# Seven block products for eight in the first FFN step of four groups: a fused linear attention and bilinear FFN kernel

## The chip, the cores and the metric

The kernel runs on one core of a Trainium2 chip. A core has a matrix engine (TensorE, in the profile PE, with its weight loads as PEld), three engines for elementwise work (VectorE or DVE, ScalarE or ACT, GpSimd or POOL), and queues that issue DMA transfers; nearly all transfers here are issued by the SP queue. Matrix products go to PSUM, which has eight banks of 128 x 512 float32; DVE and ACT read them from there. The metric is the time of one execution on the device in microseconds (us), lower is better. The kernel before takes 231.97 us (median of three executions, 231.74 to 232.61).

## The reference

Inputs are q, k, v of shape (4 batches, 8 heads, 768 positions, 64), one decay per head, and three FFN matrices. The attention goes over blocks of 64 positions and carries a state per head:

```
intra = (qb @ kb^T) * lam**(i-j), zero for j > i, then @ vb
inter = (qb * lam**(i+1)) @ kv_state
out   = intra + inter
kv_state = lam**64 * kv_state + (kb * lam**(63-j))^T @ vb
```

Its output, reordered to x with 3072 tokens and 512 columns, goes through a bilinear FFN with d_ff = 1536:

```
out = ((x @ w_a) * (x @ w_b)) @ w_out        # float32 result, 3072 x 512
```

## The kernel before, in words

**Units and groups.** The tokens are 24 blocks ("units" 0 to 23) of 128; a batch has six, and the attention state passes from unit to unit within a batch. `GROUPS` makes eight groups of 4, 1, 2, 4, 4, 4, 4 and 1 units. A group is what the FFN works on at a time: its x, transposed and in bfloat16, is the tile `xT` (four slices of 128 columns of d_model, by up to 512 tokens).

**The FFN of a group** (`ffn`). First step: for each of 12 chunks f of d_ff, four matmuls (one for each slice of d_model) accumulate `a_ps`, ACT casts it to `a_sb` (L477), four more accumulate `b_ps`, and DVE multiplies the two into `ab` (L495). The matmuls are on L468 and 512 columns wide in a group of four. Second step: for each unit t of the group, 12 matmuls over the chunks of d_ff (L515) give `op`, ACT copies it to SBUF (L510), and SP stores 128 rows of the output (L511). Rows of the first `KEEP_GROUPS` groups are kept in staging buffers instead (`o_kept`, L506) and stored later by a piece "W" (`store_kept`, L501).

**Attention pieces.** The attention of later units is done between the matmuls of the FFN. `hook(slot)` is called after each of the 12 chunks of the first step (slots 0 to 11) and after every half of an `op` in the second (slots from 12), and puts there what the written-out table `PLAN` says for the group:

- "P" (or its halves "PK" and "PV") prepares a unit: POOL multiplies k and q by powers of the decay (L276), one DMA transposes both into `qkT` (L304), and v is cast to `vb` (L295). The loads of a unit two or three further on are issued at the end of "P" (`pump`, `load_x`, L130).
- "S": eight small matmuls make the scores `kq0`, `kq1` (L332), and DVE masks them (L349, two instructions).
- "V": four matmuls update the state `kvd` (L396), and DVE copies its diagonal blocks out (`kv_copy`, L429).
- "O2", "Q": the outputs of two units (`inter` and `intra`, L366), their cast into the next group's `xT` on ACT (`evac_o`, L389), for the later units the state update too (L418), and for "Q" also the scores and masks of two more units.
- "W" stores a kept row, "C" casts a block of w_out, "T" transposes a unit on PE.

**What sets the order.** The order of all instructions is written out; each engine and the SP queue work through theirs in order, and wait on semaphores for data and for buffers. SP's order therefore mixes loads, transposes and stores: a transpose that waits for POOL holds up the loads behind it. POOL and SP run ahead of PE as far as buffers let them. PSUM has seven banks in rotation (`ps_bank`) and one for the state. Buffers that matter: `wst` (staging for weights, kept rows), `qkT`, `a_sb`, `o_sb`, and four each for raw q, k and v.

Of the kernel before, what the change touches and what calls it, by code (L numbers as in the profile page):

```python
# [22 lines left out]
def _bc(ap, dims):  # L23
# [5 lines left out]
W_CHUNKS = (256,) * 6  # L29
W_STEPS = ((0, 1), (2,), (3,), (4, 5))  # L30
W_HALVES = (4, 5)
W_BUFS = 12
LOOKAHEAD = {9: 2, 10: 1}
DMA_T = range(7, 24)
KEEP_GROUPS = 3
PACK = 4


# [2 lines left out]


PLAN = {
    0: [(0, "V", 3), (8, "C", 0), (9, "C", 1), (15, "C", 2), (18, "C", 3), (23, "PK", 4),
        (26, "C", 4), (26, "T", 4), (29, "C", 5), (29, "S", 4), (30, "PV", 4), (33, "O", 4),
        (35, "PK", 5), (35, "PV", 5)],
    1: [(0, "V", 4), (2, "T", 5), (3, "PK", 6), (6, "PV", 6), (6, "S", 5), (7, "T", 6),
        (10, "S", 6), (12, "O2", (5, 6)), (13, "P", 7)],
    2: [(0, "V", 6), (1, "P", 8), (4, "P", 9), (7, "V", 7),
        (9, "S", 7), (9, "S", 8), (6, "PK", 10), (10, "V", 8), (11, "PV", 10),  # L50
        (12, "Q", (7, 8, 9, 10)), (12, "P", 11), (13, "V", 9), (14, "P", 12),
        (14, "O2", (9, 10))],
    3: [(6, "S", 11), (6, "S", 12)],
}
for _g, _u in ((3, 11), (4, 15), (5, 19)):
    PLAN.setdefault(_g, []).extend(
        [(1, "P", _u + 2), (3, "P", _u + 3), (6 if _g == 3 else 4, "V", _u),
         (9 if _g == 3 else 7, "Q", (_u, _u + 1, _u + 2, _u + 3)), (10, "P", _u + 4),
         (12, "P", _u + 5), (13, "V", _u + 2), (16, "Q", (_u + 2, _u + 3, _u + 4, _u + 5))])
PLAN[3] += [(_s, "W", None) for _s in range(12, 19)]  # L60
PLAN[5] = [(_s, _n, (21, 22, 23) if _us == (21, 22, 23, 24) else _us)
           for _s, _n, _us in PLAN[5] if _us != 24]
PLAN[6] = [(4, "O", 23)]


@with_exitstack
def kernel(
# [11 lines left out]
    nc = tc.nc  # L79
# [13 lines left out]
    wst_pool = ctx.enter_context(tc.tile_pool(name="wst", bufs=W_BUFS))  # L93
    ld_pool = ctx.enter_context(tc.tile_pool(name="ld", bufs=4))
    prep_pool = ctx.enter_context(tc.tile_pool(name="prep", bufs=6))
    qkT_pool = ctx.enter_context(tc.tile_pool(name="qkT", bufs=5))
    msk_pool = ctx.enter_context(tc.tile_pool(name="msk", bufs=4))
    xT_pool = ctx.enter_context(tc.tile_pool(name="xT", bufs=2))
    a_pool = ctx.enter_context(tc.tile_pool(name="a", bufs=5))
    ab_pool = ctx.enter_context(tc.tile_pool(name="ab", bufs=2))  # L100
    o_pool = ctx.enter_context(tc.tile_pool(name="o", bufs=4))
    ps_pool = ctx.enter_context(tc.tile_pool(name="ps", bufs=1, space=PSUM))
    kvps_pool = ctx.enter_context(tc.tile_pool(name="kvps", bufs=1, space=PSUM))

    ctx.enter_context(tc.manual_schedule())


# [2 lines left out]
    def ps_bank(name, shape, dt, hold=False, ffn=False, at=None):  # L110
        i = bank["next"] if at is None else at
        while i in bank["held"] or (ffn and i == bank["ffn"]):
            i = (i + 1) % 7
        if ffn:
            bank["ffn"] = i
        bank["next"] = (i + 1) % 7
        if hold:
            bank["held"].add(i)
        return ps_pool.tile(shape, dt, name=name, tag=f"ps{i}")


    qr = q.rearrange("b h (nb p) d -> b nb p h d", p=BLK)
# [39 lines left out]
    def cast_w(kind, c, eng):  # L162
        t = staged.pop((kind, c))
        if kind == "o":
            dst = wo_sb[:, 2 * c:2 * c + 2, :]
        else:
            dst = w_part(wa_sb if kind == "a" else wb_sb, c)
        if eng == "act":
            nc.scalar.copy(dst, t)  # L169
        elif eng == "first":  # L170
            nc.vector.tensor_copy(dst[:, :3, :128], t[:, :3, :128])  # L171
            nc.gpsimd.tensor_copy(dst[:, 3:, :128], t[:, 3:, :128])
            nc.gpsimd.tensor_copy(dst[:, :, 128:], t[:, :, 128:])
        else:
            nc.vector.tensor_copy(dst, t)
        pump()

    pending = []
    for cs in W_STEPS:
# [8 lines left out]
    def pump():  # L188
        while pending:
            kind, c = pending[0]  # L190
            if kind in "abo":
                if len(staged) >= W_BUFS:
                    return
            elif c >= used["u"] + LOOKAHEAD.get(used["u"], 2 if used["u"] > 8 else 3):
                return
            pending.pop(0)
            if kind in "abo":
                load_w(kind, c)
            else:
                load_x(kind, c)  # L200
# [106 lines left out]
            U[u]["qT"], U[u]["kT"] = qkT[:, 0], qkT[:, 1]  # L307

    def prep_v(u):
        make_vb(u, "pool" if u < n0 + 3 else "dve")  # L310
        pump()

    def piece_T(u):
# [20 lines left out]
        return kq  # L334

    def masks(u, kq):
        ms = mask(kq)
        U[u]["m"] = lambda i, hp: ms[i][:, hp, :]

    def mask(kq, split=False):  # L340
# [94 lines left out]
    def piece_V(u):  # L435
        kv_update(u)
        if u % NB < NB - 1:
            kv_copy(u, kv["ps"])

    xTs = {}  # L440

    def pieces_O(us, nxt=()):
        kqs = [score_banks() for u in nxt]
        o_banks(us)
        for u, kq in zip(nxt, kqs):
            scores(u, kq)
        for u in us:
            inter(u)
        for b in range(2):
            for u in us:  # L450
                intra(u, b)
            evac_o(us, b)
        beside = len(us) == 2 and us[0] >= n0 + 5
        if beside:
            kv_beside(us[1])
        for u, kq in zip(nxt, kqs):
            masks(u, kq)
        if beside and us[1] % NB < NB - 1:
            kv_copy(us[1], kv["ps"])


    g_u0 = [sum(GROUPS[:i]) for i in range(len(GROUPS))]
# [36 lines left out]
    def store_kept():  # L499
        row, o_sb = kept.pop(0)  # L500
        nc.sync.dma_start(out=out_r[row], in_=o_sb)  # L501
# [66 lines left out]


    gx = {}  # L570

    def new_xT(g):
        gx[g] = xT_pool.tile([128, KS, 512], BF16, name="xT", tag="xT")
# [131 lines left out]
    for g, n in enumerate(GROUPS):  # L705
        if g + 1 < len(GROUPS):
            new_xT(g + 1)
        plan = {}
        for slot, name, us in PLAN.get(g, ()):
            plan.setdefault(slot, []).append((name, us))  # L710

        def hook(slot, plan=plan):
            for name, us in plan.get(slot, ()):
                if name == "C":
                    cast_w("o", us, "dve")
                elif name == "PK":
                    prep_k(us)
                elif name == "PV":
                    prep_v(us)
                elif name == "P":  # L720
                    prep_k(us)
                    prep_v(us)
                elif name == "W":
                    store_kept()
                elif name == "T":
                    piece_T(us)
                elif name == "S":
                    piece_S(us)
                elif name == "V":
                    piece_V(us)  # L730
                elif name == "O":
                    pieces_O((us,))
                elif name == "O2":
                    pieces_O(us)
                else:
                    pieces_O(us[:2], us[2:])

        ffn(g_u0[g], n, gx.pop(g), hook, g == 0, g + 1 == len(GROUPS))

# [1 line left out]
_INS = ['q', 'k', 'v', 'lam', 'moe_w_a', 'moe_w_b', 'moe_w_out']  # L741
# [26 lines left out]
```

## Time and profile before

| What | Value |
|---|---|
| Median of three executions | 231.97 us (231.74 to 232.61) |
| Span of the profiled execution, first to last instruction | 230.2 us |
| PE busy | 221.4 us, 96% |
| DVE, ACT, POOL busy | 118.2, 88.8, 49.9 us |
| Groups 3, 4, 5, 6 (first matmul to first matmul of the next) | 82.3, 117.6, 152.3, 187.0 to 218.8 us |
| Granted TensorE clock | 0.999 |

The time of the profiled execution itself is known by its span, 230.2 us; the 1.8 us up to the median lie around it. A page gives the busy time of each engine, the chain of waits that ended last, and groups of instructions with their mean duration and the idle time before them. The timeline gives instructions in order of time; a run of one line is merged into one row, with its count. "Releaser" is what ended a wait.

### The profile page before, as it was taken

The page shows a single profiled execution, that of the slowest core. Times are in us where ns is not written, and L with a number is a line of the kernel's source. Part 1 is how long each engine was busy: PE and PEld are TensorE (multiplying, and loading weights), DVE is VectorE, ACT ScalarE, POOL GpSimd, SP SyncE. Part 2 cuts the span into 40 slices and gives each one's busy share as a digit, 9 for nine tenths or more (in the row PEclk, how much of TensorE's full clock was granted, in tenths as well). Part 3 has the DMA queues.
Part 4 walks back from the last instruction along what each step waited for, and adds up shares of the span by engine and source line. Part 5 has one row for each costly group of instructions (what it writes and reads, how often), then busy time and mean ns, then how long its engine had stood idle before and what let it go on. Part 6 is the DMA issues. An engine that isn't in the chain of part 4 may idle for free.

```text
span 230.2 us, 4630 instructions
## 1 busy us (share of the span) xinstructions
PE 221.4 (96%) x1816; PEld 121.0 (53%) x1839; DVE 118.2 (51%) x205; ACT 88.8 (39%) x172; POOL 49.9 (22%) x65
## 2 busy tenths in 40 slices
PE   7699999999999999999999999999999999999994
PEld 2475444459688544454544454544454544444493
DVE  0994865736488845876416574426574313341050
ACT  2686563056433243242233342233342233432261
POOL 6061000228351436333302433002100000000000
PEclk9999999999999999999999999999999999999999
DMA  4999999999999999999979995249200220000211
GB/s 130 317 277 347 363 387 293 303 217 196 202 211 182 215 186 231 233 195 200 350 222 217 157 235 89 94 116 205 48 0 0 94 91 0 4 0 31 106 48 47
DMA packets 97542, 39.37 MB, mean 171 GB/s; under 512 B 85488, under 2 KB 92016, under 8 KB 97520
## 3 DMA queue, kind: packets, MB, share of 16 engines
q1 hardware_dynamic: 97232, 39.00, 75.2%
q8 instruction: 14, 0.23, 0.4%
q10 hardware_dynamic: 288, 0.07, 0.1%
q14 instruction: 8, 0.07, 0.1%
HBM read 28.32 MB, written 6.29 MB: 150 GB/s over the span
## 4 chain that ended last, share of the span: by engine, by line
PE 92%; DMA 3%; SPq 1%; issue 1%; ACT 1%; DVE 0%
PE a_ps L468 27%; PE b_ps L468 27%; PE op L515 27%; PE o_ps L366 5%; DMA k<-in_k_dram 3%; PE kq L332 3%; PE kvd L396 2%; SPq L224 1%; PE tps L318 1%; PE kq L633 1%; PE kv L396 0%; PE tk L597 0%; DVE scratch L587 0%; PE kvd L418 0%; ACT scratch L608 0%
## 5 line engine op out<-in xcount | busy, mean ns | idle before, releaser
L495 DVE TENSOR_TENSOR ab<-a_sb,b_ps 128x512 bf16<-128x512 bf16 (+2 forms) x96 | 52.2, 552 | 75.5 <-PE b_ps L468 55.1
L468 PE MATMUL a_ps<-xT,wa_sb 128*128 128x512 bf16 (+2 forms) x384 | 76.3, 322 | 0.6 <-ACT xT L389 0.3
L468 PE MATMUL b_ps<-xT,wb_sb 128*128 128x512 bf16 (+2 forms) x381 | 76.6, 325 | 0.2
L477 ACT CAST a_sb<-a_ps 128x512 bf16<-128x512 f32 (+2 forms) x96 | 45.2, 481 | 62.4 <-PE a_ps L468 60.0
L515 PE MATMUL op<-wo_sb,ab 128*128 128x512 bf16 (+2 forms) x300 | 63.9, 362 | 1.0 <-issue 0.6
L468 PEld LDWEIGHTS <-wb_sb 128*128 128x128 bf16 x384 | 34.5, 98 | 28.7 <-ACT wb_sb L169 0.2
L468 PEld LDWEIGHTS <-wa_sb 128*128 128x128 bf16 x392 | 34.4, 98 | 28.3 <-DVE wa_sb L171 0.5
L515 PEld LDWEIGHTS <-ab 128*128 128x128 bf16 x312 | 28.7, 98 | 29.9
L349 DVE TENSOR_TENSOR m<-kq,lotri 128x512 bf16<-128x512 f32 x47 | 29.3, 683 | 15.8 <-PE kq L332 15.7
L276 POOL TENSOR_TENSOR qk<-kf,lp_k 128x512 bf16<-128x512 f32 x18 | 18.8, 1042 | 73.9 <-DMA kf<-in_k_dram 60.7
L276 POOL TENSOR_TENSOR qk<-qf,lp_q 128x512 bf16<-128x512 f32 x20 | 21.9, 1097 | 22.6 <-DMA qf<-in_q_dram 22.6
L510 ACT COPY o_sb<-op 128x512 f32<-128x512 f32 (+2 forms) x19 | 10.3, 541 | 34.0 <-PE op L515 34.0
L389 ACT CAST xT<-o_ps 128x512 bf16<-128x512 f32 (+1 forms) x24 | 12.1, 555 | 17.5 <-PE o_ps L366 17.4
L429 DVE TENSOR_TENSOR st<-kvd,bdiag 128x512 bf16<-128x512 f32 x18 | 12.3, 683 | 3.2 <-PE kvd L396 3.2
L295 DVE CAST vb<-vf 128x512 bf16<-128x512 f32 x17 | 11.6, 682 | 3.8 <-DMA vf<-in_v_dram 3.7
L366 PE MATMUL o_ps<-m,vb 128*64 128x128 bf16 x192 | 8.0, 222 | 0.0
L208 PE MATMUL idle<-idle_sb 128*128 128x512 bf16 (+2 forms) x23 | 6.5, 411 | 1.3 <-DVE idle_sb L203 1.3
L295 POOL CAST vb<-vf 128x512 bf16<-128x512 f32 x7 | 4.3, 611 | 13.7 <-DMA vf<-in_v_dram 13.7
L320 ACT COPY qkT<-tps 128x1024 bf16<-128x1024 bf16 x3 | 3.0, 1012 | 10.6 <-PE tps L318 10.6
L332 PEld LDWEIGHTS <-qkT 64*128 64x128 bf16 x160 | 4.5, 94 | 4.2 <-issue 3.2
L332 PE MATMUL kq<-qkT 64*128 64x128 bf16 x160 | 6.6, 218 | 0.1
L366 PEld LDWEIGHTS <-vb 128*64 128x64 bf16 x192 | 5.8, 109 | 1.3
(58 smaller groups left out, 81.0 us busy)
## 6 DMA issues: line engine op xcount, KB each, us to landing
vf<-in_v_dram SPq DMA_DIRECT2D x24, 256.0 KB, 5.0
qf<-in_q_dram SPq DMA_DIRECT2D x20, 256.0 KB, 4.2
kf<-in_k_dram SPq DMA_DIRECT2D x20, 256.0 KB, 4.6
out_dram<-o_sb SPq DMA_DIRECT2D x16, 256.0 KB, 2.0
wst<-in_moe_w_a_dram SPq DMA_DIRECT2D x6, 512.0 KB, 8.6
wst<-in_moe_w_b_dram SPq DMA_DIRECT2D x6, 512.0 KB, 8.9
wst<-in_moe_w_out_dram SPq DMA_DIRECT2D x6, 512.0 KB, 10.6
out_dram<-o_kept SPq DMA_DIRECT2D x7, 256.0 KB, 4.0
```

Source lines behind the costliest of these rows:

```text
L276: eng_of(eng).tensor_mul(dst.rearrange("p (c b) d -> p b c d", b=2), x[:].rearrange("p (b c) d -> p b c d", b=2), lp.rearrange("p (b c) o ...
L295: eng_of(eng).tensor_copy(vb, vf)
L332: nc.tensor.matmul(kq[i][:, hp, :], lhsT=d["kT"][p, hp, :], rhs=d["qT"][p, hp, :], start=True, stop=True, skip_group_check=True)
L349: nc.vector.tensor_mul(m, kq[i], lotri_bc)
L366: nc.tensor.matmul(U[u]["o"][b][p, c // 2, :], start=new[b, h % 2], stop=True, skip_group_check=True, **ops)
L389: nc.scalar.copy(dst, src)
L429: nc.vector.tensor_mul(st[:].rearrange("p c b d -> p c (b d)"), ps[:].rearrange("p c b d -> p c (b d)"), bdiag_bc)
L468: nc.tensor.matmul(ps[:, lo:hi], lhsT=w_sb[:, s, f * 128:(f + 1) * 128], rhs=xT[:, s, lo:hi], start=(s == 0), stop=(s == KS - 1), skip_gro ...
L477: nc.scalar.copy(a_sb[:, :gt], ps[:, :gt])
L495: nc.vector.tensor_mul(ab[:, f, :gt], a_sb[:, :gt], ps[:, :gt])
L510: nc.scalar.copy(o_sb[:, lo:hi], op[:, lo:hi])
L515: nc.tensor.matmul(op[:, lo:hi], lhsT=ab[:, f, t * 128:(t + 1) * 128], rhs=wo_sb[:, f, lo:hi], start=(f == 0), stop=(f == FC - 1))
```

## The change

In groups 3 to 6 the first FFN step is no longer `ffn` but `ffn_z`. There xT is cut in two halves of 256 tokens and two halves of 256 columns of d_model, and w_a and w_b into two halves of d_model by two halves of d_ff. The product of two such 2 x 2 block matrices is formed from seven block products instead of eight. It needs sums of the blocks: four sums of each weight matrix, formed once (`weight_sum`, pieces "WS" in groups 0 and 1, eight DVE instructions), and three sums of each group's xT (`x_sums`, piece "X", three DVE instructions).

For each n of 6 (chunks n and n + 6 of d_ff at once) the seven products, each for a and b side by side in one bank (four matmuls of 256 columns), go into three banks: U takes products 1, 5, 3, 2 in turn, V takes 4 and 6, W takes 0. The banks are read while they grow: ACT copies U after product 1 (`u1`), V after product 4 (`v1`) and U after product 5 (`u2`) to SBUF; DVE forms three results as W - u1, U - v1 and V - u2; the fourth is U after product 2, cast by ACT; and one DVE multiplication of 1024 elements makes `ab` for both chunks. Product 2 and what follows it are issued one n later, inside the next one.

The second step has the same 48 matmuls, in another order: `out_part` takes first the chunks that are ready (5 and 11 last), in four banks.

Banks 0 to 4 belong to `ffn_z` in these groups, so that attention pieces there share banks 5 and 6. Buffers change: `wst` 12 to 8, `qkT` 5 to 4, `a_sb` 5 to 4, `o_sb` 4 to 3. `KEEP_GROUPS` goes from 3 to 2: five rows are kept, not seven, and stored in group 2 (slots 4, 10, 11, 12, 15), not in group 3. `PLAN` is written anew; "Q" is left in group 2 alone, and in groups 3 to 5 its parts stand as separate "S" and "O2". `KV_ENG` and `VB_ENG` say for each unit which engine copies its state and casts its v. The mask no longer has a split form in `masks`.

```diff
-W_BUFS = 12
+W_BUFS = 8
-KEEP_GROUPS = 3
+KEEP_GROUPS = 2
...
+    2: [(2, 'V', 6), (2, 'P', 8), (3, 'P', 9), (4, 'W', None), (5, 'V', 7), (5, 'PK', 10),
+        (7, 'V', 8), (8, 'S', 7), (8, 'S', 8), (10, 'V', 9), (10, 'W', None), (11, 'PV', 10),
+        (11, 'W', None), (12, 'P', 11), (12, 'W', None), (12, 'Q', (7, 8, 9, 10)),
+        (13, 'P', 12), (14, 'O2', (9, 10)), (15, 'X', 3), (15, 'P', 13), (15, 'W', None)],
+    3: [(0, 'S', 11), (2, 'P', 14), (4, 'S', 12), (7, 'S', 13), (7, 'P', 15),
+        (9, 'O2', (11, 12)), (11, 'S', 14), (11, 'V', 13), (15, 'P', 16),
+        (16, 'O2', (13, 14)), (16, 'X', 4), (17, 'P', 17), (17, 'P', 18), (17, 'S', 15),
+        (19, 'S', 16), (19, 'P', 19)],
...
+    def weight_sum(i):
+        kind, j = "ab"[i % 2], i // 2
...
+        if j == 0:
+            nc.vector.tensor_sub(z[:, 0], a22, a21)
+        elif j == 1:
+            nc.vector.tensor_sub(z[:, 1], a11, z[:, 0])
+        elif j == 2:
+            nc.vector.tensor_sub(z[:, 2], a12, z[:, 1])
+        else:
+            nc.vector.tensor_add(z[:, 3], a11, a21)
...
+    def x_sums(g):
...
+        nc.vector.tensor_sub(z_sub, xT[:, :, 0:256], xT[:, :, 256:512])
+        nc.vector.tensor_add(z_add, xT[:, 0:2, :], xT[:, 2:4, :])
+        nc.vector.tensor_add(z_mix, xT[:, 0:2, 0:256], xT[:, 2:4, 256:512])
...
+        def product(ps, n, i, fresh=False):
+            for k, kind in enumerate("ab"):
+                wt = lhs(kind, i)
+                for s in range(2):
+                    nc.tensor.matmul(ps[:, k, :], lhsT=wt[:, s, n * 128:(n + 1) * 128],
+                                     rhs=rhs[i][:, s, :], start=(fresh and k == 0 and s == 0),
+                                     stop=True, skip_group_check=True)
+
+        def snap(ps, tag):
+            t = wst_pool.tile([128, 2, 256], F32, name=tag, tag="wst")
+            nc.scalar.copy(t, ps)
+            return t
...
+        def finish(n):
+            d = P.pop(n)
+            product(d["U"], n, 2)
+            oab = d["oab"]
+            nc.scalar.copy(oab[:, 0], d["U"])
+            o5 = oab[:].rearrange("p (h t) k c -> p h t k c", h=2)
+            nc.vector.tensor_mul(
+                ab[:].rearrange("p (h i) (t c) -> p h i t c", h=2, t=2)[:, :, n],
+                o5[:, :, :, 0, :], o5[:, :, :, 1, :])
+
+        def begin(n):
+            d = P[n] = {}
+            d["U"] = z_bank("U", n % 2)
+            product(d["U"], n, 1, True)
+            d["u1"] = snap(d["U"], "u1")
+
+        for n in range(NP):
+            if n != 1:
+                begin(n)
+            d = P[n]
+            oab = d["oab"] = wst_pool.tile([128, 4, 2, 256], BF16, name="oab", tag="wst")
+            d["V"] = z_bank("V", 2 + n % 2)
+            product(d["V"], n, 4, True)
+            v1 = snap(d["V"], "v1")
+            hook(2 * n)
+            W = z_bank("W", 4)
+            product(W, n, 0, True)
+            nc.vector.tensor_sub(oab[:, 2], W, d["u1"])
+            product(d["U"], n, 5)
+            u2 = snap(d["U"], "u2")
+            if n:
+                finish(n - 1)
+            else:
+                begin(1)
+            product(d["V"], n, 6)
+            product(d["U"], n, 3)
+            nc.vector.tensor_sub(oab[:, 1], d["U"], v1)
+            nc.vector.tensor_sub(oab[:, 3], d["V"], u2)
+            hook(2 * n + 1)
...
+        out_part(0, early[:3])
+        finish(NP - 1)
+        out_part(0, early[3:])
+        hook(FC)
+        out_part(1, early)
```

## The prediction

> **What bounds the kernel now.** First the page's first part and the chain that ended last, which say that PE is the path.
>
> ```profile
> PE 221.4 (96%) x1816; PEld 121.0 (53%) x1839; DVE 118.2 (51%) x205; ACT 88.8 (39%) x172; POOL 49.9 (22%) x65
> PE 92%; DMA 3%; SPq 1%; issue 1%; ACT 1%; DVE 0%
> ```
>
> So time is won by taking PE work away, and lost by making PE wait. How long PE takes for a step is read from the chain in order of time: start, duration, count.
>
> ```profile
> 62.34 0.44 PE a_ps L468 x4
> ...
> 82.27 0.86 PE a_ps L468 x4
> ...
> 105.34 2.59 PE op L515 x12
> ```
>
> Four matmuls take 0.864 us at 512 columns (82.27 to 83.14) and 0.437 us at 256 (62.34, group 2): 216 and 109 ns each, so halving the width costs nothing extra. The third line is the second step, 216 ns a matmul. Then what DVE and ACT need, from the groups by shape (line, engine, tiles, count, busy us, mean ns; then the idle time before them):
>
> ```profile
> L349 DVE TENSOR_TENSOR m<-kq,lotri 128x512 bf16<-128x512 f32 x47 | 29.3, 683 | 15.8 <-PE kq L332 15.7
> ...
> L510 ACT COPY o_sb<-op 128x512 f32<-128x512 f32 x16 | 9.4, 585 | 32.1 <-PE op L515 32.1
> ...
> L495 DVE TENSOR_TENSOR ab<-a_sb,b_ps 128x256 bf16<-128x256 bf16 x12 | 5.0, 418 | 5.1 <-ACT a_sb L477 3.0 <-PE b_ps L468 1.8
> ...
> L587 DVE TENSOR_TENSOR scratch<-k,lp_k 128x512 bf16<-128x512 f32 x4 | 2.8, 692 | 0.3
> ```
>
> and how closely they follow each other, from the timeline:
>
> ```profile
> 34.69 2.04 ACT L477 CAST a_sb<-a_ps 128x512 bf16<-128x512 f32 x4
> ...
> 82.11 1.03 PE L468 MATMUL a_ps<-xT,wa_sb 128*128 128x512 bf16 x4
> 83.17 0.59 ACT L477 CAST a_sb<-a_ps 128x512 bf16<-128x512 f32 x1 [0.23 <-PE a_ps L468]
> ...
> 95.07 2.48 DVE L349 TENSOR_TENSOR m<-kq,lotri 128x512 bf16<-128x512 f32 x4
> ```
>
> A DVE instruction on 512 elements lasts 0.68, but four in a row take 2.48, so one starts (2.48 - 0.68) / 3 = 0.60 after the other; on ACT (2.04 - 0.59) / 3 = 0.49. ACT starts 0.20 after PE could go on (a_ps ends at 83.14, the next matmul began at 82.97). Last, the end of group 2 in the timeline:
>
> ```profile
> 70.05 1.23 SPq L304 DMA_TRANSPOSE qkT<-qk  x1
> ...
> 71.34 0.58 SPq L130 DMA_DIRECT2D qf<-in_q_dram  x1
> ...
> 78.65 2.00 SPq L304 DMA_TRANSPOSE qkT<-qk  x1
> ...
> 81.93 0.54 DVE L295 CAST vb<-vf 128x512 bf16<-128x512 f32 x1 [2.42 <-DMA vf<-in_v_dram]
> ```
>
> DVE waits there 2.42 us for unit 12's v; nothing on PE needs DVE then.
>
> **The change part by part.** *PE in the first step.* Before, 24 quartets of 0.864 = 20.73 us a group; after, 6 x 7 products of 0.437 = 18.35. Saved 2.38, in four groups **9.5 us**. The second step keeps its 48 matmuls, attention its own.
>
> *One n of the steady state*, from the durations above (t = 0 at product 1; 3.06 on PE if nothing waits). PE: U1 0 to 0.44, V4 to 0.87, W0 to 1.31, U5 to 1.75, the former n's U2 to 2.19, V6 to 2.62, U3 to 3.06. ACT: u1 0.64 to 1.22, v1 1.13 to 1.71, u2 1.95 to 2.53, the former U's cast 2.44 to 3.02. A release reaches PE about 0.05 later (DVE to PE at 10.77 and 10.82). U5 needs u1 at 1.27 and starts at 1.31; U3 needs u2 at 2.58 and starts at 2.62; the next U1 needs its bank at 3.07 and could start at 3.06. All fit, by 0.04 or -0.01. DVE: the multiplication starts at about 3.1, U - v1 0.6 later, done at 4.4; the next U2 needs it at 4.81: 0.4 to spare. ACT starts 4 x 0.49 = 1.96 in 3.06, DVE 4 x 0.60 = 2.4. Margins of 0.04 won't all hold; bounds 0 and 0.26 a cycle (a late read each at U5, U3 and U1, 0.05 to 0.1); taken 0.025 x 24 = **0.6** lost.
>
> *The multiplication* of 1024 bfloat16, both inputs in SBUF, is in no row. By bytes it is the float32 instruction of L587 (0.69), by elements 0.69 + 512 x 1.05 ns = 1.22 (1.05 is the slope from 0.418 at 256 to 0.684 at 512). I take 0.69: the nearest row with two SBUF inputs reads as many bytes. The same holds for x_sums (0.69, 0.69, 0.42) and the eight weight sums of 1536 (0.96 or 1.76).
>
> *The end of the first step.* U2 of the last n comes after three op matmuls, 0.65, not after 1.75, but needs U - v1 at 1.35 after U3's end: 0.70 late, less what the hook of slot 11 puts between (S14 and V13 0.5, S19 0.3, nothing, O 0.6): 0.2 + 0.4 + 0.7 + 0.1 = **1.4** lost. ab of chunks 5 and 11 is then 1.6 away, and 17 matmuls (3.7) cover it.
>
> *The start of group 3.* In the changed order z_sub stands on DVE behind the cast of unit 12's v, and V4, PE's second product, needs z_sub. In before v arrives at 81.93 and group 3 starts at 82.27. Two kept rows now stand in SP's queue before unit 11's loads: the first fits the wait before 70.05, the second moves the loads from 71.34 by about 0.5 (one of L501 issues in 0.52), and its 256 KB take some 0.7 of busy DMA. So v12 at 82.4 to 83.2, cast 0.42, z_sub 0.69: V4 at 83.6 to 84.3 in place of 82.7. Lost **1.2** (0.7 to 1.8; 0 if the stores find idle DMA, 4 if all five rows' 1.3 MB at 200 GB/s came before). S11, at slot 0, needs unit 11's transpose: issued at 78.65 + 0.5 to 1.2, and transposes land 3.1 to 5.9 later, median 4.3: 83.5 to 84.2, just inside the same stall. ACT likewise waits for unit 11's v at slot 12, ahead of xT's casts; PE needs those only at group 3, and ACT has 2 us to spare.
>
> *Attention in the first steps.* Each S adds 0.30 to PE and 1.2 to DVE, each O2 1.2 to PE and 1.0 to ACT. DVE starts in group 3 up to slot 10: 24 x 0.60, three S 3.6, one state copy 0.6: 18.6, against PE 20.5; groups 4 and 5, 18.5 and 18.0 against 21.6 and 20.4. There is room, but DVE instructions with both inputs in SBUF meet POOL:
>
> ```profile
> 91.24 1.32 DVE L295 CAST vb<-vf 128x512 bf16<-128x512 f32 x1 [1.27 <-DMA vf<-in_v_dram]
> ...
> 91.24 1.04 POOL L276 TENSOR_TENSOR qk<-qf,lp_q 128x512 bf16<-128x512 f32 x1
> ```
>
> That cast lasts 0.42 alone and 1.32 beside POOL. POOL's 22 of these for units 13 to 23 take 23 us of about 100, so some 4 of 18 multiplications wait about 0.7, of which 0.4 is spare (0 if none meet, 4 x 1.04 = 4 at most). With state copies on ACT before u1 (0.2 once): **1.2** lost. [...]
>
> *Groups 0 to 2.* Weight sums: in 39.6 to 53.5 DVE is busy 8.0 of 13.9 us, and five starts of 0.87 go in; two stand before the last w_out cast, which then ends at 43.6 + 2 x 0.87 + 0.7 = 46.0, while its matmuls start near 48; unit 5's k moves from 49.35 to 51.9, needed by a transpose at 52.9. In group 1 three more, between multiplications of 0.2 with four a_sb ahead. **0.3** lost; by elements, without this cover, 2.5. The smaller pools cost nothing: w_a's fifth block needs the buffer that POOL's cast frees at 18.7 and is issued at 21.0; eight transfers stay outstanding; uncovered, it would be one 512 KB block, 1.5. The stores leave group 3, where nothing waited for them.
>
> *Preparations* of units 13 to 23 move by up to a dozen slots, each with two POOL multiplications, a transpose on SP and three loads behind it. POOL and SP run ahead of PE as before. With four qkT buffers a transpose waits on SP for the outputs of the unit four before, and loads and stores stand behind it: unit 19's waits for slot 5 of group 4, takes 2.0 to issue and 4.3 to land, and S19 comes 9 us after that slot. The least room has S16 (slot 19; its transpose follows the store of slot 15), 6.7 us for 0.9 + 4.3. At nothing; if landing takes 5.9 or more there, up to 1.
>
> Sum: 9.5 - 0.6 - 1.4 - 1.2 - 1.2 - 0.3 = 4.8 saved. 230.2 - 4.8 = 225.4 span; the median lies 1.8 above the profiled span: **227.2**.
>
> **The rivals.** *A, slower: elements, not bytes.* If bfloat16 pairs go one by one, each multiplication takes 1.13 of DVE's starts, not 0.60. DVE then has 21.8, 21.7, 21.2 and 18.8 against PE's 20.5, 21.6, 20.4 and 18.7: with about 0.8 of filling each, some 5 lost; weight sums 2.2 and x_sums 0.5 more: 227.2 + 7.7 = **234.9**. It decides from 4.8 lost, about 0.95 a multiplication. For it: no DVE row here handles two bfloat16 SBUF inputs; against it: 1024 float32 are cast in 0.69 (L175). [...]
>
> *B, about the same: the reads are late.* If U5, U3 and U1 wait 0.07 each, the cycle is 3.27, not 3.06: 24 x 0.21 = 5 more than none, 4.4 more than taken: **231.6**. For it: margins of 0.04, and three round trips a cycle. Against it: the times repeat to 0.01 in before (a_sb idles 1.14 again and again).
>
> *C: the start of group 3 waits longer*, for transpose 11 or v12: 4, not 1.2: **230.0**. For it: DMA is at nine tenths throughout.
>
> *D, better: nothing waits* but the ends (1.4) and 0.6 elsewhere: **224.5**.
>
> **How the numbers follow.** Main case 0.58 (225.2 to 229.5), D 0.10, C 0.11, B 0.11, A 0.10. Half a per cent, 1.2 us, is about what a measurement can tell from no change: faster means below 230.8. Main, D, most of C, a little of B: 0.77. Within: most of B, some of C: 0.09. Slower: A and the rest of B: 0.14. Range 224.5 to 232.6: outside lie A and the far half of D.
>
> **What would show it.** In the profile after: quartets of 0.437 on PE with 18.4 to 19.5 us a first step without attention; the multiplication at about 0.69; one wait of 0.7 to 1.8 for z_sub at the start of group 3 and none later; U2 of the last n waiting for DVE. Wrong if DVE is busy above 90% of the first steps, if ACT's copies release PE in every cycle, or if PE waits at the start of group 3 for over 3 us.

## The result, and the profile after

The changed kernel takes 228.3 us (median of four runs, 228.1 to 228.7) where the kernel before takes 232.0 (231.7 to 232.6): a ratio of 0.984, 95% interval 0.982 to 0.986. Predicted were 227.2, with a range of 224.5 to 232.6. The profiled execution went from 230.2 to 227.0 us, so 3.2 were saved where the sum of the prediction has 4.8; the profiled one is the longest of the four, and by the medians 3.7 were saved. On another chip the same kernel gave 0.981 (0.978 to 0.983). Ratios leave out executions over 1.5% longer than the shortest of their kernel on that chip, which here are one of `sums_in_gaps` and one of the kernel before beside it.

First the page of the changed kernel: busy time of each engine, then the chain that ended last, by engine.

```profile
PE 217.8 (96%) x2127; PEld 148.3 (65%) x2127; DVE 154.6 (68%) x257; ACT 117.0 (52%) x233; POOL 59.2 (26%) x73
PE 77%; DMA 8%; SPq 6%; DVE 4%; issue 2%; ACT 1%; ACTq 0%; DVEq 0%
```

PE is still the engine that is busy throughout. Its share of the chain fell from 92% to 77%, but this share says little about what is lost: it was 87% when the same kernel ran again, and 73% in the fastest version below. Then the new multiplication, from the groups by shape and from the list of its tile (least, median and greatest duration in ns):

```profile
L658 DVE TENSOR_TENSOR ab<-oab 128x1024 bf16<-128x1024 bf16 x24 | 18.8, 783 | 9.1 <-ACT oab L656 9.0
...
L658 DVE TENSOR_TENSOR ab<-oab x24: 674/692/1355, 91.1 to 206.5; 128x1024 bf16<-128x1024 bf16 x24
```

Alone it lasts 0.69, as taken; the mean of 0.78 comes from five of the 24, at 0.99 to 1.36, each beside work on POOL. Next one cycle of the steady state in group 6, from the timeline (start, duration, engine and line; PE's rows are half products, and "..." stands for rows left out):

```profile
191.33 0.38 PE L641 MATMUL U<-xT,wz_a 128*128 128x256 bf16 x2
...
192.03 0.59 ACT L647 COPY u<-U 128x512 f32<-128x512 f32 x1 [0.78 <-PE U L641]
...
192.66 0.38 PE L641 MATMUL U<-z_mix,wz_a 128*128 128x256 bf16 x2
...
193.78 0.59 ACT L656 CAST oab<-U 128x512 bf16<-128x512 f32 x1
...
194.40 0.69 DVE L658 TENSOR_TENSOR ab<-oab 128x1024 bf16<-128x1024 bf16 x1 [0.64 <-ACT oab L656]
194.42 0.38 PE L641 MATMUL U<-xT,wz_a 128*128 128x256 bf16 x2
```

From U1 to the next U1 it is 3.09 where PE alone needs 3.06; U5 starts 0.04 after u1 has ended. The worst place lies ahead of the changed first steps, in group 1; first three rows of the kernel before, then the changed kernel (both from the timelines):

```profile
49.35 0.92 DVE L276 TENSOR_TENSOR qk<-kf,lp_k 128x512 bf16<-128x512 f32 x1
...
52.89 0.61 PE L318 MATMUL tps<-ident,qk 128*128 128x128 bf16 x8
...
56.01 0.61 PE L318 MATMUL tps<-ident,qk 128*128 128x128 bf16 x8
```

```profile
52.09 0.94 DVE L216 TENSOR_TENSOR wz_a<-wa_sb,wz_a 128x1536 bf16<-128x1536 bf16 x1
52.23 1.70 POOL L318 TENSOR_TENSOR qk<-kf,lp_k 128x512 bf16<-128x512 f32 x1 [1.75 <-DMA kf<-in_k_dram]
52.96 1.53 DVE L318 TENSOR_TENSOR qk<-kf,lp_k 128x512 bf16<-128x512 f32 x1
...
54.54 0.40 PE L360 MATMUL tps<-ident,qk 128*128 128x128 bf16 x4 [0.49 <-DVE qk L318]
...
56.59 1.46 DVE L216 TENSOR_TENSOR wz_b<-wb_sb,wz_b 128x1536 bf16<-128x1536 bf16 x1
...
58.30 0.61 PE L360 MATMUL tps<-ident,qk 128*128 128x128 bf16 x8 [0.61 <-DVE ab L537]
...
61.56 1.46 PE L557 MATMUL op<-wo_sb,ab 128*128 128x512 bf16 x6 [0.15 <-DVE ab L537]
```

Unit 5's k is multiplied at 52.96 (at 49.35 before, and 51.9 by the prediction) and lasts 1.53 beside POOL; PE waits for it, and twice more for an ab that stands on DVE behind a weight sum. In before PE has no wait in this stage. And the entry to group 3:

```profile
82.94 1.25 DVE L337 CAST vb<-vf 128x512 bf16<-128x512 f32 x1 [1.54 <-POOL qk L318]
...
84.56 0.69 DVE L620 TENSOR_TENSOR z_sub<-xT 128x1024 bf16<-128x1024 bf16 x1 [0.36 <-ACT xT L431]
...
85.00 0.38 PE L641 MATMUL U<-xT,wz_a 128*128 128x256 bf16 x2
...
85.43 0.38 PE L641 MATMUL V<-z_sub,wa_sb 128*128 128x256 bf16 x2
...
98.16 0.40 PE L374 MATMUL kq<-qkT 64*128 64x128 bf16 x8 [0.32 <-DMA qkT<-qk]
```

V4 follows U1 at once: the wait predicted there does not occur; the first one in group 3 is S13's, for its transpose.

Where the time went, by stage, worked out from the timelines. A stage runs from the first product of its first step to the next stage's; starts are those of the timeline, 82.11 for group 3 of the kernel before, where the chain has 82.27. The last two columns are of the runs below.

| Stage (us) | Before | After | After, again | Sums alone in before | Fastest run |
|---|---|---|---|---|---|
| start of group 1 | 51.33 | 52.07 | 51.77 | 51.33 | 51.49 |
| group 1 | 10.85 | 12.99 | 12.61 | 12.91 | 10.88 |
| group 2 | 19.93 | 19.94 | 19.93 | 20.30 | 20.14 |
| group 3 to the end | 148.1 | 142.0 | 141.7 | 147.8 | 141.6 |
| profiled span | 230.2 | 227.0 | 226.0 | 232.4 | 224.1 |

So from group 3 on 6.1 us are won, 1.0 more than the 5.1 of the prediction's terms, and 2.9 are lost before, where it has 0.3.

### The profile page after: what moved, and what is told of

It reads as the page before. It is cut to its first block, busy times and chain, and to the rows that moved or that the text cites. A ratio compares the mean times of both kernels' runs of the same rounds, so it can differ in the third digit from the quotient of the medians.

```text
span 227.0 us, 5349 instructions
## 1 busy us (share of the span) xinstructions
PE 217.8 (96%) x2127; PEld 148.3 (65%) x2127; DVE 154.6 (68%) x257; ACT 117.0 (52%) x233; POOL 59.2 (26%) x73
## 4 chain that ended last, share of the span: by engine, by line
PE 77%; DMA 8%; SPq 6%; DVE 4%; issue 2%; ACT 1%; ACTq 0%; DVEq 0%
PE op L697 18%; PE U L641 15%; PE b_ps L510 9%; PE op L557 9%; PE a_ps L510 7%; PE V L641 7%; PE o_ps L408 4%; DMA wst<-in_moe_w_b_dram 4%; PE W L641 4%; SPq L154 3%; DMA qkT<-qk 3%; PE kq L374 2%; DMA q<-in_q_dram 2%; PE kvd L438 1%; SPq L183 1%
## 5 line engine op out<-in xcount | busy, mean ns | idle before, releaser
L697 PE MATMUL op<-wo_sb,ab 128*128 128x512 bf16 x192 | 43.3, 379 | 0.0
L647 ACT COPY u<-U 128x512 f32<-128x512 f32 x48 | 27.8, 587 | 18.7 <-PE U L641 17.9
L537 DVE TENSOR_TENSOR ab<-a_sb,b_ps 128x128 bf16<-128x128 bf16 (+2 forms) x48 | 19.3, 415 | 20.9 <-ACT a_sb L519 13.6
L510 PE MATMUL b_ps<-xT,wb_sb 128*128 128x128 bf16 (+2 forms) x192 | 27.6, 272 | 1.2 <-DVE wb_sb L199 1.0
L510 PE MATMUL a_ps<-xT,wa_sb 128*128 128x128 bf16 (+2 forms) x200 | 27.7, 268 | 0.0
L658 DVE TENSOR_TENSOR ab<-oab 128x1024 bf16<-128x1024 bf16 x24 | 18.8, 783 | 9.1 <-ACT oab L656 9.0
L557 PE MATMUL op<-wo_sb,ab 128*128 128x512 bf16 (+2 forms) x120 | 22.5, 337 | 0.2 <-DVE ab L537 0.2
L510 PEld LDWEIGHTS <-wb_sb 128*128 128x128 bf16 x192 | 15.8, 98 | 7.7 <-DVE wb_sb L199 1.5
L510 PEld LDWEIGHTS <-wa_sb 128*128 128x128 bf16 x200 | 16.0, 98 | 6.7 <-DVE wa_sb L199 0.4
L641 PEld LDWEIGHTS <-wz_b 128*128 128x128 bf16 x192 | 18.7, 97 | 2.2
```

What stands on the lines that cost most here:

```text
L510: nc.tensor.matmul(ps[:, lo:hi], lhsT=w_sb[:, s, f * 128:(f + 1) * 128], rhs=xT[:, s, lo:hi], start=(s == 0), stop=(s == KS - 1), skip_gro ...
L537: nc.vector.tensor_mul(ab[:, f, :gt], a_sb[:, :gt], ps[:, :gt])
L557: nc.tensor.matmul(op[:, lo:hi], lhsT=ab[:, f, t * 128:(t + 1) * 128], rhs=wo_sb[:, f, lo:hi], start=(f == 0), stop=(f == FC - 1))
L641: nc.tensor.matmul(ps[:, k, :], lhsT=wt[:, s, n * 128:(n + 1) * 128], rhs=rhs[i][:, s, :], start=(fresh and k == 0 and s == 0), stop=True, ...
L647: nc.scalar.copy(t, ps)
L658: nc.vector.tensor_mul(ab[:].rearrange("p (h i) (t c) -> p h i t c", h=2, t=2)[:, :, n], o5[:, :, :, 0, :], o5[:, :, :, 1, :])
```

## The experiments

Ratios are to the kernel before, run on the same chip, with 95% intervals.

**1. Do the weight sums cost 2 us?** `before_weight_sums` is the kernel before with the smaller `wst` and two kept groups, so five stores in group 3 and not seven, and with the eight sums, whose results nothing uses. The other buffers stay as in before.

```diff
-W_BUFS = 12
+W_BUFS = 8
-KEEP_GROUPS = 3
+KEEP_GROUPS = 2
 PLAN[0]: +(27, "WS", 0) (28, "WS", 1) (31, "WS", 2) (32, "WS", 3) (34, "WS", 4)
 PLAN[1]: +(4, "WS", 5) (8, "WS", 6) (11, "WS", 7)
 PLAN[3]: 'W' at slots 12 to 18 -> 12 to 16
```

> The kernel before, with the smaller pools of after (8 weight buffers, two groups' blocks kept) and the eight weight sums at the slots of after, their results unused; the first steps are as before. Prediction's step: the sums cost 0.3, so 232.3. Reading of the trace of after: they cost 2.1 in group 1, and the late start of group 1 another 0.7, so 234.1 to 234.9; 1 us of it may be given back where groups 2 and 3 waited for loads: 233.1 at least.

Measured: 234.1 (233.6 to 234.4), ratio 1.007 (1.005 to 1.010), which is 1.7 us (1.1 to 2.3), not the 0.3 of the prediction; the profile is 2.2 longer than that of before. Group 1 has the waits of the changed kernel, at the same instructions (timeline, PE's waits):

```profile
53.75 0.40 PE L339 MATMUL tps<-ident,qk 128*128 128x128 bf16 x4 [0.45 <-DVE qk L297]
...
57.48 0.61 PE L339 MATMUL tps<-ident,qk 128*128 128x128 bf16 x8 [0.58 <-DVE ab L516]
...
60.74 1.46 PE L536 MATMUL op<-wo_sb,ab 128*128 128x512 bf16 x5 [0.15 <-DVE ab L516]
```

In this profile group 1 is 2.06 longer and group 2 0.4. Group 1 starts at 51.33, as in before, so the sums and the smaller `wst` cost its start nothing here; over all kernels run here that start lies anywhere from 51.1 to 52.1, and the 0.7 of the changed kernel's profile lies within this scatter.

How much the sums cost depends on which of DVE and POOL comes first. Seven profiles have the sums at these slots. In four (`after`, `after_again`, `pool_none`, `before_weight_sums`) POOL's multiplication for unit 6 starts 0.1 to 0.8 before that of unit 5's k on DVE; the latter lasts 1.52 to 1.53, PE waits 0.35 to 0.49 for it, and group 1 takes 12.6 to 13.0. In three (`act_extra`, `u1_late`, `place_only`) DVE starts first or at the same time; k lasts 0.68, PE does not wait for it, and group 1 takes 12.0. A second meeting adds to it: the sum at 56.59 takes 1.43 to 1.50 in the three longest of the seven and 1.13 to 1.17 in the others. So the sums cost 1.1 to 2.2 in group 1, and what lies between is such meetings.

**2. Are they better elsewhere?** `ws_in_group2` moves sum 2 to slot 11 of group 1 and 3 to 7 into group 2; `ws_and_stores_later` also moves the stores of group 2.

```diff
 PLAN[0]: -(31, 'WS', 2) (32, 'WS', 3) (34, 'WS', 4)
 PLAN[1]: -(4, 'WS', 5) (8, 'WS', 6) (11, 'WS', 7)   +(11, 'WS', 2)
 PLAN[2]: +(0, 'WS', 3) (1, 'WS', 4) (3, 'WS', 5) (6, 'WS', 6) (7, 'WS', 7)
# ws_and_stores_later, besides
 PLAN[2]: -(4, 'W', None) (10, 'W', None)   +(11, 'W', None) (11, 'W', None)
```

> The kernel after, with the weight sums 2 to 7 moved: sum 2 to slot 11 of group 1, sums 3 to 7 to slots 0, 1, 3, 6 and 7 of group 2. Theory (from the trace of after): the sums in group 1 hold up unit 5's k on DVE and with it PE's transposes; away from there group 1 lasts 10.9 us again instead of 13.0, so stage starts from group 2 on come 2.1 earlier; then group 3 starts before unit 12's v and transpose 11 are there and waits 1.0 to 1.5 for them, as the prediction had it. Total 227.2 to 227.8 against 228.3 for after. Rival (the start of group 3 has no such wait): the whole 2.1 is kept, 226.2. Second rival (group 1 is long for another reason than the sums): no change, 228.3.

> The same, and the stores of weight blocks in group 2 are taken behind the loads of units 11 and 12 (slots 11 and 12 instead of 4 and 10). Theory: the wait at the start of group 3 is made by the stores that stand before those loads, so 0.5 to 1.2 of the 1.0 to 1.5 goes: 226.3 to 227.0. Rival (DMA as a whole is late, not the place in the queue): as with the sums moved alone, within 0.3.

Measured: 229.1, ratio 0.986 (0.982 to 0.990), and 229.5, 0.988 (0.985 to 0.991). The first is longer than any of its expectations; the second, 0.4 above the first, is longer than its theory's 226.3 to 227.0. In both group 1 lasts 10.87, with all the smaller buffers of the changed kernel, so the sums make its excess and the buffers do not. But group 2 grows from 19.94 to 22.14 and 23.75. In the first of them (timeline):

```profile
70.94 0.38 PE L439 MATMUL kvd<-vb,qk 128*128 128x128 bf16 x4 [0.67 <-DVE st L472]
...
74.53 0.60 PE L511 MATMUL a_ps<-xT,wa_sb 128*128 128x256 bf16 x4 [0.52 <-DVE ab L538]
```

DVE is busy there from 63.8 to 78 without a gap, and PE waits for a state copy and an ab in its queue; in the second run the wait for the state copy is 2.44. The theory had expected this gain to be lost at the start of group 3; it was lost in group 2, so these two runs do not yet tell about that start. For the stores they tell one thing: v12 was cast at 82.13, where it was cast at 84.33 with the stores in front.

**3. Sums where DVE is idle.** `sums_in_gaps` puts them into DVE's gaps; `gaps_and_start3` also takes the cast of v12 behind the sums over xT, and S11 and S13 later.

```diff
 PLAN[0]: (7, 'WS', 0) (7, 'WS', 2) (7, 'WS', 4) (27, 'WS', 6) (28, 'WS', 1) (35, 'WS', 3) (35, 'WS', 5)
 PLAN[1]: (13, 'WS', 7)
# gaps_and_start3, besides
 PLAN[2]: (13, 'P', 12) -> (13, 'PK', 12) ... (15, 'X', 3), (15, 'PV', 12)
 PLAN[3]: (0, 'S', 11) -> (2, 'S', 11);  (7, 'S', 13) -> (8, 'S', 13)
```

> The kernel after, with the eight weight sums only where DVE stood idle in the runs so far: three at slot 7 of group 0 (DVE idle from 34.5 to 37.6), two at slots 27 and 28, two behind unit 5's multiplication at slot 35 (idle from 50.5 to 52.9), one at slot 13 of group 1 (idle from 61.6 to 63.8). Theory: group 1 lasts 10.9 and group 2 19.9, so group 3 starts near 82.5 and now meets the predicted wait: z_sub stands on DVE behind the cast of unit 12's v, which comes at 83 to 84.3, so V4 waits 0.7 to 2.0. Total 226.9 to 228.2 against 228.3 for after. Rival (unit 12's v comes earlier too, since group 2 runs earlier): no wait, 226.0 to 226.4.

> The same, and unit 12's v is cast on DVE behind the three sums over xT (its place moves from slot 13 to slot 15 of group 2), S11 comes at slot 2 of group 3 instead of 0, and S13 at slot 8 instead of 7. Theory (the wait at the start of group 3 is z_sub behind that cast, then transposes 11 and 13): it goes, and 225.8 to 226.4 is left. Rival (transposes and loads are late whatever the order on DVE and PE): the wait moves to S11 or S12, and the time is within 0.4 of the sums in gaps alone.

Measured: the first took 227.9 and 228.3 in two executions and 230.7 to 231.6 in four, ratio 0.989 (0.984 to 0.995); the second took 228.5, 0.983 (0.980 to 0.986), where 225.8 to 226.4 were expected. Group 1 is 10.87 again, without a price in group 0. But group 2 grows to 21.3 and 20.9, and now the predicted wait stands at the start of group 3 (timeline of the sums in gaps, its longest execution):

```profile
72.32 0.40 PE L374 MATMUL kq<-qkT 64*128 64x128 bf16 x8 [1.23 <-DMA qkT<-qk]
...
84.33 0.54 DVE L337 CAST vb<-vf 128x512 bf16<-128x512 f32 x1 [4.52 <-DMA vf<-in_v_dram]
84.79 1.53 DVE L620 TENSOR_TENSOR z_sub<-xT 128x1024 bf16<-128x1024 bf16 x1
86.38 0.53 PE L641 MATMUL V<-z_sub,wa_sb 128*128 128x256 bf16 x2 [2.37 <-DVE z_sub L620]
86.70 0.63 PE L641 MATMUL V<-z_sub,wb_sb 128*128 128x256 bf16 x2
```

The scores of unit 8 wait 1.23 for their transpose in group 2. DVE waits 4.5 for v12, z_sub meets POOL (1.53, not 0.69), and V4 waits 2.37. Then something that no theory had: the half products that follow last 0.53 to 0.64, not 0.38. The granted clock of these stretches shows why; the columns are the stretch, its length, busy time and count on PE, PEld, DVE, ACT and POOL, the granted clock, DMA's share and GB/s.

```profile
83.80:86.38 2.58, 0.21 (x3) 0.04 (x2) 2.05 (x3) 1.28 (x3) 1.97 (x2) 1.00 1.13 184
86.38:88.40 2.02, 2.02 (x15) 1.17 (x15) 1.37 (x3) 0.59 (x1) 0.00 (x0) 0.52 1.30 235
88.40:90.00 1.60, 1.60 (x10) 1.16 (x8) 1.40 (x3) 0.27 (x1) 1.19 (x2) 0.54 1.12 341
90.00:92.00 2.00, 2.00 (x21) 1.79 (x19) 0.74 (x2) 1.27 (x3) 1.41 (x2) 1.00 1.14 238
```

After the pause PE ran 3.6 us at a clock of 0.52 to 0.54, some 1.7 us lost on top of the wait. The four executions of 230.7 and more have a mean clock of 0.991 to 0.993 and the two others 1.0, which fits such a stretch in each of the four; whether the two others had the wait is not known, and their times are those of the changed kernel (227.6 to 228.7). With the cast moved, z_sub is on time, but z_add and z_mix meet POOL (1.53 and 1.26) and PE waits 0.72 and 0.59 for them, beside 0.82 for the scores of unit 8 in group 2 and 0.45 later in group 3. So what group 1 won is lost again in waits further on, and the time is that of the changed kernel (0.981 to 0.984).

**4. What do POOL's collisions cost?** `pool_none` leaves out POOL's multiplications of units 13 to 23.

```diff
 def make_ks(u, eng):
+    if u >= 13:
+        raw.pop((u, "k"))
+        qk = U[12]["qk"]
+        U[u] = dict(qk=qk, kn=qk[:, 1])
+        return
 def make_qs(u, eng):
+    if u >= 13:
+        raw.pop((u, "q"))
+        return
```

> The kernel after without POOL's multiplications of q and k for units 13 to 23 (left out: the scaling of these units' q and k; their transposes and products take unit 12's). Theory: POOL and DVE collisions make the stalls of groups 3 and 4 (1.2 and 1.2 to 1.5 us) and a little in group 6; without POOL all 24 multiplications on DVE last 0.69, group 3 and 4 stall for 0.2 to 0.5 each, and the total falls by 1.5 to 2.5, to 225.8 to 226.8. Rival (the stalls come from DVE's and ACT's own order, a cast or a state copy in front of a read): multiplications at 0.69, yet the total falls by less than 0.5.

Measured: 227.4, ratio 0.979 (0.976 to 0.983), not told apart from the changed kernel's 0.984 and 0.981. The multiplication is now at 0.70 on the mean (groups by shape):

```profile
L666 DVE TENSOR_TENSOR ab<-oab 128x1024 bf16<-128x1024 bf16 x24 | 16.8, 699 | 9.7 <-ACT oab L664 9.6
```

DVE is relieved of 2.0 us in these 24, and group 3 to the end takes 141.1 where it took 142.0, and 141.7 when the changed kernel ran again: 0.6 to 0.9 less, between theory (1.5 to 2.5) and rival (below 0.5). Part of it is S13's transpose: PE waited 0.39 for it in the changed kernel, 0.08 when that ran again, and not at all here. So the collisions are there, and most of them hide behind DVE's spare time.

**5. How close are ACT's reads?** Two copies of 64 columns in each n, one in front of U1's end, one behind it; both results are unused.

```diff
 def begin(n):
     ...
+    nc.scalar.copy(idle_sb[:, :64], idle_sb[:, 64:128])    # act_extra
+    nc.scalar.copy(idle_sb[:, :64], d["U"][:, 0, :64])     # u1_late, in its place
     d["u1"] = snap(d["U"], "u1")
```

> The kernel after with one more copy of 64 columns on ACT ahead of u1 in each n (24 in all, some 0.2 us each by ACT's smaller rows; results unused). The prediction's cycle has ACT 0.04 ahead of PE at U5, U3 and the next U1. If those margins are that small, nearly all of the 0.2 goes onto PE in each cycle: 24 x 0.15 to 0.2 = 3.5 to 5 us more than after, 231.8 to 233.3. Rival (the margins are wider, PE waits only where U1's bank is late): less than 1.5 us more, below 229.8.

> The kernel after with a copy of 64 columns of the U bank on ACT between PE's U1 and u1, so that u1 (and v1 behind it) starts some 0.15 to 0.25 later in each of the 24 n; its result is unused. The copy in front of it, which ran in ACT's idle time before U1 was ready, cost nothing. Theory (the margin at U5 is the 0.04 to 0.08 of the prediction's cycle): U5 waits 0.1 to 0.2 in each n, 24 x 0.1 to 0.2 = 2.4 to 4.8 more, 230.7 to 233.1. Rival (PE has other work queued that covers it): under 1 more.

Measured: 228.1, ratio 0.983 (0.978 to 0.987), and 229.2, 0.988 (0.986 to 0.990). The first costs nothing, though each copy lasts 0.26: it runs while ACT waits for U1. That was a weak test, since u1 itself was not late. The second makes u1 0.10 late (timeline):

```profile
192.09 0.21 ACT L666 CAST idle_sb<-U 128x64 bf16<-128x64 f32 x1 [0.78 <-PE U L641]
192.19 0.59 ACT L647 COPY u<-U 128x512 f32<-128x512 f32 x1
...
192.84 0.38 PE L641 MATMUL U<-z_mix,wz_a 128*128 128x256 bf16 x2
```

W0's second half began at 192.48 and takes 0.22, so U5 is 0.14 late, and the cycle 3.20. On the whole it costs about 1, under the 2.4 to 4.8 expected, since not every n shows it: in this profile U5 is 0.08 to 0.14 late in 11 of the 24 n, 1.3 in all, where the changed kernel has one n over 0.02 (0.30). So ACT has time to spare, but the reads come just in time: in these 11 n a delay of 0.10 on ACT comes out on PE whole or nearly so.

**6. A faster version.** `gaps_later` has the sums in the gaps, puts the stores behind the loads of units 11 and 12 and asks for S8 and S11 to S14 later; `gaps_later_s14` mends the places of S13 and S14; `place_only` has its placement with the sums where the changed kernel has them; `after_again` is the changed kernel.

```diff
 PLAN[2]: 'W' at slots 4, 10, 11, 12, 15 -> 11, 11, 11, 12, 15;  (8, 'S', 8) -> (10, 'S', 8)
 PLAN[3]: (0, 'S', 11) -> (2, 'S', 11);  (4, 'S', 12) -> (6, 'S', 12);  (9, 'O2', (11, 12)) -> (10, ...)
# gaps_later:     (7, 'S', 13) -> (9, 'S', 13);  (11, 'S', 14) -> (13, 'S', 14)
# gaps_later_s14: (7, 'S', 13) -> (8, 'S', 13)
```

> The weight sums in the gaps, as before; the kept rows' stores of group 2 behind the loads of units 11 and 12 (slots 11, 11, 11, 12, 15); S8 at slot 10 of group 2 instead of 8; in group 3 S11 at slot 2, S12 at 6, S13 at 9, O2 of 11 and 12 at 10, S14 at 13. Theory (the entry to group 3 is set by the order of loads, stores and transposes in SP's queue, and by attention that asks for transposes early): unit 12's v is cast by 82.2, z_sub waits only for xT, group 3 starts near 82.0 and has no wait over 0.5; 225.6 to 226.6. Rival (the DMA engines, busy nine tenths, set the pace of groups 2 and 3 whatever the order): waits for transposes 7 to 13 of 1.5 to 3 in all stay somewhere between 70 and 100 us, and the time is 227.5 to 229.

> The kernel with the sums in the gaps and the late stores, with S13 of group 3 at slot 8 and S14 at slot 11 (in the run before, O2 of units 11 and 12 followed S13 by one slot and waited 1.45 us for the bank that S13's mask on DVE set free, and S14 in the second step added its own). Theory (that wait was one of position, not of transfers): group 3's first step falls by 1.2 to 1.5, and the time is 0.9 to 1.5 below the run before, 226.5 to 227.5; z_sub's collision with POOL (1.53 instead of 0.69) may stay. Rival (transposes 13 and 14 are late then, since DMA is full): S13 or S14 waits as long, no gain, 228.

> The kernel after, unchanged, beside it on the same chip: 228.3, start of group 1 anywhere between 51.2 and 52.1 as in the other runs, group 1 of 12.0 to 13.0, no wait over 0.5 at the start of group 3.

> The kernel after with the late stores and the places of S8 and S11 to S14 of the fastest run, but with the weight sums where after has them. Theory (two limits stand one behind the other: the sums hold group 1 up, and the loads, stores and transposes hold the entry to group 3 up; taking away either alone brings nothing, both together 1.8): group 1 lasts 12.0 to 13.0, group 3 has no wait, and the time is within 0.5 of after, 227.9 to 228.7. Rival (the placement alone brought the gain): 226.5 to 227.2.

Measured: `gaps_later` 228.3, ratio 0.984 (0.982 to 0.987), in the rival's range but without the waits for transposes that the rival names. It had a wait of 1.26 for a z_sub that met POOL, and waits of 1.06 and 0.39 of unit 11's and 12's outputs for S13's mask, one slot ahead of them. With the two places mended: 226.7 (225.8 to 228.4), ratio 0.975 (0.972 to 0.979), beside 228.5 (227.6 to 228.7), 0.981 (0.978 to 0.983), for the changed kernel on the same chip; the intervals just touch. Its entry to group 3 (timeline):

```profile
80.03 0.43 DVE L338 CAST vb<-vf 128x512 bf16<-128x512 f32 x1 [1.12 <-DMA vf<-in_v_dram]
...
82.07 0.69 DVE L621 TENSOR_TENSOR z_sub<-xT 128x1024 bf16<-128x1024 bf16 x1 [1.61 <-ACT xT L432]
...
82.51 0.38 PE L642 MATMUL U<-xT,wz_a 128*128 128x256 bf16 x2
...
82.95 0.38 PE L642 MATMUL V<-z_sub,wa_sb 128*128 128x256 bf16 x2
```

v12 is cast two microseconds before z_sub, group 3 starts 1.8 to 2.5 earlier than in the changed kernel, and PE waits for nothing there. The placement alone gave 227.3, ratio 0.979 (0.977 to 0.982). That lies between theory (227.9 to 228.7) and rival (226.5 to 227.2), nearer to the rival; its interval overlaps both that of the changed kernel (0.978 to 0.983) and that of both edits together (0.972 to 0.979). Its profile is 1.4 shorter than that of `after_again`, but by stages only 0.1 of this lies where the edit acts: 0.36 less from group 3 on, 0.22 more in group 2. The rest is the start of group 1 (51.1) and group 1 (12.0), which the edit does not touch and which scatter.

So moving the sums alone brought nothing (0.983 to 0.989), because the 1.1 to 2.2 won in group 1 came back as waits in groups 2 and 3, and with the placement mended too the time is about 1.8 shorter. That one limit stands behind the other is shown in this direction. That the placement alone is worth nothing is not shown: by the medians it is 1.0 to 1.2 shorter than the changed kernel, on another chip, and the intervals do not decide it.

## Why the prediction was right, and where it was wrong

The sign, the main case and most sizes held. That the total came so near is in part luck: 2.6 more was lost ahead of group 3 and 1.7 more on PE around attention than the sum has, and against that the waits at the start of group 3 and at the end of the first steps, 2.6 in the sum, cost 0.3 to 0.6.

*PE's saving, 9.5, and what attention does to it.* Products run at the 0.437 taken. From the start of each PE instruction to the next, the four first steps take 83.4 us in before and 76.1 after: 7.3 saved. PE's waits there are 0.9: S13's transpose 0.39, one late u1 0.29, one U2 0.23. Most of the rest is a cost that the prediction had at nothing: in after 16 pieces of scores (64-row matmuls) or outputs stand right behind a product, and each such change costs PE 0.09 to 0.10 beyond the piece's own time; in before five do. That is 1.1. The state updates, whose matmuls are 128 x 128, cost no such time: in after the one at 124.93 starts 0.22 after the half product ahead of it, as the next half product would, and the product behind it 0.22 after that. And the scores of a unit, now done singly, take 0.33, where two in one place took 0.55: 0.6 more over 13 of them. Both show in PE's rows, of before and after (a row's start is to be set against the next one's):

```profile
93.33 1.03 PE L468 MATMUL b_ps<-xT,wb_sb 128*128 128x512 bf16 x4
94.29 0.62 PE L332 MATMUL kq<-qkT 64*128 64x128 bf16 x16
94.84 1.04 PE L468 MATMUL a_ps<-xT,wa_sb 128*128 128x512 bf16 x4
```

```profile
91.77 0.38 PE L641 MATMUL V<-z_sub,wb_sb 128*128 128x256 bf16 x2
92.09 0.40 PE L374 MATMUL kq<-qkT 64*128 64x128 bf16 x8
92.42 0.39 PE L641 MATMUL W<-z_add,wa_sb 128*128 128x256 bf16 x2
```

The two half-width products of the last three rows take 0.22, so the scores could start at 91.99 and start 0.10 later; from there to W0 it is 0.33. "Each S adds 0.30" was right, but its term counted only what DVE and POOL make late.

*Steady state, 0.6 lost.* About right: cycles of 3.07 to 3.09, some 0.3 over 24, so rival B with its 3.27 falls. One u1 was 0.34 late for a reason that the trace does not show, and cost 0.29; it was as late in the same n of group 6 when the kernel ran again.

*The multiplication at 0.69.* Right: 692 ns at the median of the 24, where L587 of the kernel before, with as many bytes, has 692 on the mean and the estimate by elements 1.22; so rival A falls.

*End of the first step, 1.4 lost.* Too much: the second steps took about 0.5 longer. U2 of the last n waited 0.34 in group 4 (0.56 when run again) and at most 0.04 in the others; in group 3 the three op matmuls and the pieces between covered it. For group 5 the prediction put "nothing" between and took 0.7, the largest part of its sum; that was misread, for `PLAN` has O2 of units 21 and 22 at slot 11 there, and it stood on PE from 173.31 on and covered the wait.

*Start of group 3, 1.2 lost.* Not in the changed kernel, for a reason outside the step: group 2 ended 2.9 later than in before, and that covered v12. The mechanism is the one named, z_sub behind the cast of unit 12's v and behind stores in SP's queue: once the sums were moved it stood there with 2.37, over the bound of 1.8, since the step had not counted z_sub's collision with POOL (0.84 of the 2.37), and the clock took 1.7 more. The share of the stores is shown by the two runs of experiment 2, which differ in them alone: v12 cast at 84.33 and at 82.13. S11, expected just inside the stall, did not wait; S13, which the step did not name, was the one that did (0.39 beyond a change's usual 0.10).

*Attention and POOL, 1.2 lost.* 0.6 to 0.9 by the run without POOL. Five multiplications met POOL, where the step has four of 18; the longest, at 137.48, lasts 1.35 beside POOL, against 0.69 at the median of the 24. The row that the prediction showed for it is of a cast, which has one input; this one has two. The step's subtractions, which read a PSUM bank, last 0.67 to 0.69 each, also beside POOL (138.76). DVE was relieved of 2.0 us and the end came 0.6 to 0.9 earlier, so that a late multiplication mostly meets spare time.

*Groups 0 to 2, 0.3 lost.* This is the step that failed: 2.9 in the profile, of which 2.1 (1.8 when run again, and 1.1 in three variants) lie in group 1 and the rest is scatter. Durations by bytes were right: 0.94 to 0.95 alone. Its "two stand before the last w_out cast" and "unit 5's k moves from 49.35 to 51.9" counted each sum at 0.87; beside POOL they took up to 1.46, and the multiplication of k, taken at 0.92, took 1.53 at 52.96, too late for a transpose at 54.1; at 0.92 it would have been in time. Its "three more, between multiplications of 0.2 with four a_sb ahead" overlooked that PE's transposes in group 1 wait for those multiplications (0.61 at 58.30, and 0.32 in the variants where group 1 takes 12.0). The collisions were priced in groups 3 to 5 and not here, where POOL is busiest (10.5 of 13.0 us in group 1).

*Preparations and smaller pools, 0.* Right as far as it shows: PE does not wait for S16, and with the sums moved group 1 takes 10.87 to 10.88, as in before, with all the smaller pools.

Together, with the breaks (1.1), the scores (0.6), PE's waits in the first steps (0.9), the cycle (0.3) and the second steps (0.5): 9.5 - 1.1 - 0.6 - 0.9 - 0.3 - 0.5 = 6.1 from group 3 on, less 2.9 before it, is the 3.2 of the two profiles. A loss of the size of rival C's, 2.8, was there, but ahead of group 3. D needed the sums out of the way, and `gaps_later_s14` came 1.6 us nearer to it than the changed kernel; in its profile PE waits only once after 60 us, 0.7 for the last U2 of group 4, and yet it is 2.2 above D's 224.5, since D too has nothing for the breaks and the single scores. How much of the entry to group 3 is the order in SP's queue and how much a DMA at nine tenths was not tried further.

## What to carry to other kernels

Work that prepares a cheaper algorithm is paid where it is placed: eight instructions of 0.95 on a half-idle engine cost 1 to 2 us of the path in one order and, in groups 0 and 1, none in another, so look for that engine's gaps in the timeline, and price what stands behind the work, not its share of the stage. A stage that runs late hides the next wait: when a repair brings nothing, compare stage by stage, for the gain may have been lost one stage further on, and the next limit has to be taken away with the first. Count each piece of scores or outputs that is put between two steady products as a break of its own, here 0.09 to 0.10 us.

## What the hardware showed that was not expected

A pause of PE of 2.4 us was followed once by 3.6 us at a granted clock of 0.52 to 0.54; another pause of 2.44 us (in `ws_and_stores_later`, ended at 72.19) and one of 1.26 (in `gaps_later`) were followed by a full clock. So this wait was followed by a further loss of some 1.7 us. That the pause caused it is not shown: mean clocks of 0.991 to 0.993 were also granted in two other executions of `ws_and_stores_later`, which took only 0.1 to 0.2 us longer than the rest, and 0.993 in one of the kernel before (235.4 us), and none of these was profiled.

Collisions between DVE and POOL lengthened either side: in the changed kernel POOL's 1.04 became 1.49 to 1.81 and the sum of 1536 elements went from 0.94 to 1.46, and in `sums_in_gaps` z_sub's 0.69 became 1.53. In the changed kernel POOL's multiplication, begun at 52.23, ends at 53.93, and unit 5's k, begun on DVE at 52.96, ends 0.56 after it; POOL's next one, begun at 53.90, ends 0.90 after that. How the two share the time is not shown.
